# Rank products of four-tile groups, a gate product and one narrowing operation put at other places of a hand-written order

## The chip, the cores and the metric

The kernel runs on one core of a Trainium2 chip. The metric is device time in microseconds (us), the median of three runs. The core has a matmul engine (PE, with its weight loads as PEld), a vector engine (DVE), a scalar engine (ACT), GpSimd (POOL) and SyncE (SP), which mostly issues transfers (DMA). Each engine works through its own instructions in order and waits for the others on semaphores.

## What is computed

A gated linear attention over 4 batches, 8 heads, 768 positions of width 40; then a mixture of 8 experts (3072 tokens of width 320), of which each token takes at most one; then a block with three weights, a maximum over the three products, and an output product.

```python
# attention, per head and position t
m_new = maximum(f + m, i)
C = exp(f + m - m_new) * C + exp(i - m_new) * outer(v, k)
n = exp(f + m - m_new) * n + exp(i - m_new) * k
y = sigmoid(o) * (C @ q) / maximum(abs(n @ q), 1)
# experts: only tokens with x @ w_skip > 0
e = argmax(xc @ w_gate); gate = softmax(xc @ w_gate)[e]
out = xc + gate * (maximum(xc @ w1[e], 0) @ w2[e])
# final block
h = maximum(maximum(x @ w1, x @ w2), x @ w3)
return h @ w_out
```

## The kernel before, in words

**Tiles and turns.** The attention is cut into 6 chunks of 128 positions times 4 batches: 24 tiles, numbered 0 to 23, tile i being chunk i // 4 and batch i % 4. The loop `for i in range(NT)` (L1221) is a software pipeline; one pass is called a turn here. Nothing reorders it: each engine's instructions stand in the order in which the code emits them. Turn i holds, in this order,
- SP's loads of tile i+2 (`load`, TP at L872 and KP at L874) and of the gate rows;
- `score(i+1)` (PE L900, with DVE's products W, L908) and `keys(i+1)` (POOL kt, L915);
- the previous tile's `last` (POOL XR, L988);
- `state_mm(i)` (PE L929), the first half of `pv_mm` (PE L965), `expo_mm` (PE L882, L890, ACT L891), `inter_mm` (PE L936);
- `state(i)`: DVE xi (L946), POOL Cst (L949: the state of one batch times its decay), DVE Cst (L954: two adds onto it);
- the second half of `expo_mm`, then rank and gate products when they are due, then the second half of `pv_mm`;
- `logit` (PE L1015), `trans(i-1)` (PE L1000: the previous tile's XR is transposed into bank mi, ACT xTH L1002 and DVE xTL L1005 read it);
- a scatter (POOL L1118) if one is pending, two in turns 20 and later;
- a *weave*: several runs of small DVE operations, one operation of each in turn: `finish` (DVE xs L972, den L978 to L982, then POOL g L985), `narrow`, xTL (L1005), and what the routing or the gates need.

A turn in the trace is taken below from the first L900 of `score(i+1)` to the next one's. Turn 6 begins at 55.38 us, turn 16 at 129.46, turn 20 at 155.98, turn 21 at 161.72, turn 22 at 171.98; the first product of the final block (L322) is at 181.69.

**Routing.** Tiles 0 to 15 are routed in groups of four, tiles 16 to 23 in pairs. When a group's logits are there, its next turns run `route2` (DVE: which expert) and then `route3_mm` and `route3` (L1080 to L1107): PE sums one-hot rows into each token's rank among its expert's tokens, in bank mi; ACT copies the ranks (rk); five small DVE operations make the row numbers si and the place column of XR; POOL adds the group's counts to cum (L1091). Then each tile of the group is scattered: an indirect DMA that writes 128 rows of `table` in device memory. After the attention the experts gather their tokens from `table`.

**The early read.** In turn 20 `early_load` (SP L289) reads 512 rows of `table`, those of tokens that take no expert, for the final block, whose first products are put into the last turns. The rows that it needs come from the first 12 tiles (`assert issued[0] >= SNAP`). It is the only read of `table` in the attention.

**Narrowing.** Weights of the final block come in as pieces of 128x384 double-width numbers (mraw, DMA issued by ACT, L210). DVE packs a piece into single width in three operations: L224, L226 and, a turn later, L239 (`narrow2`). ACT then takes the high part (mH, L246), POOL the remainder (mL or oL, L252, `mp.low`, called behind `state`).

**Gates.** For the next chunk a gate product (`gating3`, PE L848 to L850 into bank mi, ACT copies KG and DEC, L851 and L852) comes once in four turns: turns 5, 9, 13, 17 from the second chunk on.

Of the kernel before, what the change touches and what calls it, by code (L numbers as in the profile page):

```python
# [20 lines left out]
NC = S // NB  # L21
# [30 lines left out]
def bc(ap, shape):  # L52
    return ap.to_broadcast(shape)
# [587 lines left out]
def attention(k, tp, kp, og, gates, w9, wts, left, mp, moe):  # L641
    tc, nc = k.tc, k.nc
    rows, table, ident, zrow = k.rows, k.table, k.ident, k.zrow
    with ExitStack() as ctx:
# [291 lines left out]
                    nc.tensor.matmul(t["pi"][:, 2 * j : 2 * j + 2].rearrange("p a d -> p (a d)"), t["TP"][:, 0, j],  # L936
                                     Cst[:, b, j], start=True, stop=True)

        def state(i):
            t = st[i]  # L940
            c, b = t["c"], t["b"]
            Cb = Cst[0:104, b]
            pc = t["pc"]
            if c > 0:
                t["xi"] = xi = pt2.tile([128, H, D1], F32, name="xi", bufs=1)
                nc.vector.tensor_mul(xi, t["pi"], bc(KG[c % 2][:, 1, b * H : (b + 1) * H].unsqueeze(2), [128, H, D1]))  # L946
            if c < NC - 1:
                if c > 0:
                    nc.gpsimd.tensor_mul(Cb, Cb, bc(DEC[c % 2][:, b].unsqueeze(2), [104, 4, 2 * D1]))  # L949
                for q in range(2):  # L950
                    r = slice(64 * q, 64 * q + D)
                    w = Cb[r, :, q * D1 : (q + 1) * D1]
                    if c > 0:
                        nc.vector.tensor_add(w, w, pc[r])  # L954
                    else:
                        nc.vector.tensor_copy(w, pc[r])
# [193 lines left out]
                todo.append(r)  # L1150

        todo = []
        rts = [None, None]


        early = {}
# [64 lines left out]
        for i in range(NT):  # L1221
            c = i // B
            if i > 0 and i + 2 < NT:
                load(i + 2)
            if i % B == 2 and c + 1 < NC:
                loado(c + 1)
            if i % B == 0 and 0 < c and c + 1 < NC:
                rowout(c + 1)
            if B <= i + 3 < NT:
                rowin(i + 3)  # L1230
            if i == 1:
                w9load()
            if i == 3:
                w9split()
            if i < E:
                pads(i)
            if i == NT - 4:
                early_load()
            rts = [todo.pop() if todo else None, rts[0]]
            if i + 1 < NT:  # L1240
                score(i + 1)
                keys(i + 1)
            if i > 0:
                st[i - 1]["last"]()
            state_mm(i)
            pv_mm(i, 0)
            if i == NT - 1:
                tail2(i - 2)
                rts[0] = todo.pop()
            if i == NT - 2:  # L1250
                early_prep(0)
                early_prep(1)
            if i + 2 < NT:
                expo_mm(i + 2, 0)
            if i + 1 == NT:
                early["run"] = mixed_block(k, mp, early["x"], early["xt"], T2, early_tile)
                fill(1)
            inter_mm(i)
            state(i)
            mp.low()  # L1260
            if rts[0]:
                route2_mm(rts[0])
            if i + 2 < NT:
                expo_mm(i + 2, 1)
            if i == 0:
                sigm(0)
            if rts[1] and i < NT - 2:
                route3_mm(rts[1])
            if i % B == 1 + (c == 0) and c + 1 < NC:
                gating3(c + 1)  # L1270
            if i % B == 3 and c + 1 < NC:
                sigm(c + 1)
            pv_mm(i, 4)
            if rts[1] and i >= NT - 2:
                route3_mm(rts[1], "pl" if i == NT - 1 else "mi")
            if 1 < i < NT - 1:
                tail2(i - 2)
            if i > 0:
                tail1(i - 1)
            mp.load(min(i + 1, 4))  # L1280
            scatter()
            if i >= NT - B:
                scatter()
            runs = [finish(i, xr(i)), mp.narrow(PIECES[i])]
            if i > 0 and "low" in st[i - 1]:
                runs.append(st[i - 1]["low"])
            if i % B == (c == 0) and c + 1 < NC:
                runs.append(gating2(c + 1))
            if i == NT - 1:
                fill(2)  # L1290
                weave(*runs[:2])
                next(st[i - 1]["low"])
                st[i]["last"]()
                fill(1)
                tail1(i)
                fill(1)
                runs = [st[i]["low"]]
            if rts[0]:
                runs.append(route2(rts[0]))
            if rts[1]:  # L1300
                runs.append(route3(rts[1]))
            if i % B == (c == 0) and c + 2 < NC:
                runs.append(gating(c + 2))
            if i % B == 1 + (c == 0) and c + 2 < NC:
                runs.append(gating1(c + 2))
            if i == NT - 2:
                next(runs[0])
                next(st[i - 1]["low"])
                early_prep(2)
                early_prep(3)  # L1310
            weave(*runs)
            if i % B == (c == 0) and c + 2 < NC:
                gload(c + 3)
# [81 lines left out]
```

## Time and profile before

| | us |
|---|---|
| median of three runs | 587.95 (586.24, 587.95, 590.15) |
| profiled execution | 588.96 |
| its span, first to last instruction | 587.2 |
| attention, turns 6 to 20 | 55.38 to 161.72 |
| turns 21 and 22 | 161.72 to 181.69 |
| turn 23 and what is left of the routing, beside the first final blocks | 181.69 to 206.00 |
| experts | 206.00 to 340.00 |
| the final block | 340.00 to 587.20 |

Over the span PE is busy 547.4 us (93%), DVE 314.1 (53%), ACT 235.6, POOL 229.0. An average over stages says little: what an edit is worth is read in its own stage. In the rows below a time is the instruction's start; the number in brackets is how long its engine stood idle before it, and behind the arrow is what released it. DMA-issuing instructions of SP and ACT are marked SPq and ACTq.

### The profile page before, as it was taken

The numbers are of one execution on the slowest core, as the hardware profiler recorded it, in microseconds if no ns is written. First come the engines' busy times: TensorE is split into PE (matmuls) and PEld (weight loads), VectorE is DVE, ScalarE is ACT, GpSimd is POOL, SyncE is SP. The second block draws the span as 40 slices with busy tenths as digits, with TensorE's granted clock in tenths as the row PEclk, the third lists the DMA queues.
The fourth block names the chain that finished last, engine by engine and source line by source line (L and its number), as shares of the span: only waits on it lengthen the run. The fifth ranks groups of instructions, "written<-read, shape, count | busy, mean of one in ns | idle before, by whom it ended". The sixth has DMA issues, their size and how long they took to land.

```text
span 587.2 us, 10688 instructions
## 1 busy us (share of the span) xinstructions
PE 547.4 (93%) x3890; PEld 478.1 (81%) x3890; DVE 314.1 (53%) x786; ACT 235.6 (40%) x505; POOL 229.0 (39%) x271
## 2 busy tenths in 40 slices
PE   7978988989979998999999999999999999999990
PEld 4866777777868778999999988898898898898890
DVE  7768989998866673677787532312212311311210
ACT  5554645554622333768677422221222222222120
POOL 4325667687754442242424412131231232132231
PEclk9989988999979999999999999999999999999996
DMA  6687877687740137569887511010001001000000
GB/s 224 179 284 229 285 232 221 221 271 226 237 150 23 47 110 249 171 196 308 250 284 251 157 56 55 0 46 1 1 35 56 1 33 58 1 24 23 0 25 27
DMA packets 38631, 77.01 MB, mean 131 GB/s; under 512 B 6446, under 2 KB 20783, under 8 KB 38568
## 3 DMA queue, kind: packets, MB, share of 16 engines
q1 hardware_dynamic: 27528, 57.33, 30.9%
q10 hardware_dynamic: 8064, 9.05, 5.1%
q0 software_dynamic: 2976, 9.85, 4.4%
q8 instruction: 33, 0.54, 0.4%
q14 instruction: 30, 0.25, 0.1%
HBM read 63.30 MB, written 13.27 MB: 130 GB/s over the span
## 4 chain that ended last, share of the span: by engine, by line
PE 71%; DVE 11%; DMA 7%; issue 3%; POOL 3%; ACT 2%; SPq 0%; ACTq 0%; POOLq 0%; DVEq 0%
PE pd L322 17%; PE ps L322 17%; PE pd L471 6%; PE pv L965 3%; PE ps L404 3%; DMA mraw<-m 2%; DMA SA<-rows 2%; DMA TP<-tp 2%; PE pv L426 1%; PE pv L428 1%; PE ic L427 1%; PE ic L428 1%; PE ic L426 1%; PE pv L427 1%; PE ps L900 1%
## 5 line engine op out<-in xcount | busy, mean ns | idle before, releaser
L303 POOL TENSOR_TENSOR hL<-t,hH 128x512 fp32r<-128x512 f32 x30 | 38.6, 1288 | 141.5 <-ACT hH L302 141.5
L161 DVE TENSOR_TENSOR w<-raw,w 128x768 fp32r<-128x768 f32 (+1 forms) x48 | 48.5, 1037 | 14.3 <-ACT w L160 14.3
L965 PE MATMUL pv<-KP,W 128*128 128x123 f32 (+2 forms) x384 | 55.2, 290 | 0.1
L302 ACT CAST hH<-t 128x512 fp32r<-128x512 f32 x30 | 18.6, 621 | 90.5 <-DVE t L312 90.5
L160 ACT CAST w<-raw 128x768 fp32r<-128x768 f32 (+1 forms) x64 | 49.2, 786 | 13.3 <-DMA raw<-w 8.2
L965 PEld LDWEIGHTS pv<-KP,W 128*128 128x128 f32 x384 | 49.8, 200 | 3.4 <-DVE xs L972 0.4
L311 DVE TENSOR_TENSOR t<-t,ps 128x512 f32<-128x512 f32 x15 | 10.3, 688 | 64.3 <-PE ps L322 64.2
L322 PE MATMUL ps<-fxH,mH 128*128 128x512 f32 x108 | 43.3, 401 | 0.0
L322 PE MATMUL pd<-fxH,mH 128*128 128x512 f32 x108 | 43.0, 399 | 0.0
L322 PE MATMUL ps<-fxH,mL 128*128 128x512 f32 x108 | 42.8, 396 | 0.0
L322 PE MATMUL pd<-fxH,mL 128*128 128x512 f32 x108 | 42.8, 396 | 0.0
L985 POOL TENSOR_TENSOR g<-O,den 128x320 f32<-128x320 f32 x24 | 19.9, 829 | 58.1 <-DVE den L982 36.0
L891 ACT ACTIVATE W<-pd 128x512 f32<-128x512 f32 x48 | 27.9, 592 | 27.5 <-PE pd L890 21.3
L471 PE MATMUL pd<-xT,w 128*128 128x256 f32 x288 | 37.8, 283 | 0.0
L900 PE MATMUL ps<-TP 64*128 64x128 f32 x384 | 30.7, 301 | 6.5 <-DMA TP<-tp 4.3
L471 PEld LDWEIGHTS pd<-xT,w 128*128 128x128 f32 x288 | 35.4, 188 | 0.2 <-DVE hL L475 0.2
L900 PEld LDWEIGHTS ps<-TP 64*128 64x128 f32 x384 | 25.8, 201 | 11.0 <-DVE den L982 3.0
L432 POOL DMA_INDIRECT table<-y,xb x14 | 14.3, 1023 | 52.2 <-DMA raw<-w 13.5
L161 POOL TENSOR_TENSOR w<-raw,w 128x640 fp32r<-128x640 f32 x16 | 25.2, 1580 | 20.1 <-ACT w L160 20.0
L908 DVE TENSOR_TENSOR W<-ps,W 128x512 f32<-128x512 f32 x48 | 30.5, 675 | 1.4 <-PE ps L900 1.0
L344 POOL DMA_INDIRECT out<-o,fx x20 | 19.6, 982 | 28.4 <-ACT o L343 26.9
L1118 POOL DMA_INDIRECT table<-XR,si x24 | 24.6, 1023 | 11.6 <-DVE xi L946 5.2
(376 smaller groups left out, 1498.0 us busy)
## 6 DMA issues: line engine op xcount, KB each, us to landing
TP<-tp SPq DMA_DIRECT2D x24, 512.0 KB
raw<-w SPq DMA_DIRECT2D x32, 384.0 KB
raw<-w SPq DMA_DIRECT2D x32, 320.0 KB
KP<-kp SPq DMA_DIRECT2D x24, 324.0 KB
mraw<-m ACTq DMA_DIRECT2D x18, 384.0 KB
O<-og SPq DMA_DIRECT2D x6, 640.0 KB
fx<-table SPq DMA_DIRECT2D x5, 642.0 KB
table<-zrow SPq DMA_DIRECT2D x8, 323.0 KB
```

What stands on the lines that cost most here:

```text
L160: nc.scalar.copy(hi, r)
L161: (nc.gpsimd if m and s % 2 else nc.vector).tensor_sub(lo, r, hi.bitcast(F32))
L303: nc.gpsimd.tensor_sub(g, t, h.bitcast(F32))
L322: nc.tensor.matmul(p, w, z, start=i == 0, stop=i == len(tt) - 1)
L344: ins = nc.gpsimd.indirect_dma_start(k.out, bass.IndirectOffsetOnAxis(ap=x.bitcast(I32)[:, j + q, IDC : IDC + 1], axis=0), o, None, bounds ...
L471: nc.tensor.matmul(ps[:, f], w, x, start=f == 0 and i == 0, stop=f == 1 and i == 7)
L891: nc.scalar.activation(st[i]["W"][:, q], pd, AF.Exp)
L900: nc.tensor.matmul(ps[q][:, j], TP[r, 1, j], TP[r, 0, j], start=True, stop=True)
L908: nc.vector.tensor_mul(t["W"][:, q], t["ps"][q], t["W"][:, q])
L965: nc.tensor.matmul(t["pv"][:, h:h1], t["W"][:, h % 2, h // 2], t["ve"][:, h:h1], start=True, stop=True)
L985: nc.gpsimd.tensor_mul(g, sg[c][:, b], bc(den.unsqueeze(2), [128, H, D]))
L1118: ins = nc.gpsimd.indirect_dma_start(table, bass.IndirectOffsetOnAxis(ap=si, axis=0), x, None, bounds_check=ROWS - 1, oob_is_err=False)
```

## The change

- The rank products (`route3_mm`) and the DVE work behind them (`route3`) of a group of four come a turn later: in turns 8, 12, 16 and 20, where they stood in 7, 11, 15 and 19. In that turn the rank products stand right behind `score` and `keys`, ahead of `state_mm`; before, they stood behind the second half of `expo_mm`. Groups of two keep their turns.
- The scatters follow: those of tiles 0 to 15 come a turn later, and from turn 19 on (one turn sooner) two may go in a turn. So tiles 10 and 11 both go in turn 19, turn 20 has no scatter (before, those of tiles 12 and 13), and turns 21 and 22 have the two each of the next group.
- `gating3` stands in turns 6, 10, 14 and 18, where it stood in 5, 9, 13 and 17.
- `narrow` is made ahead of `state`, and its first operation, an L239 where a piece is half packed, comes between xi and the state's adds (turns 4 to 21, 18 times). The rest of its operations move one place up in the weave. A piece that leaves the list sooner lets `mp.load` fetch the following one a turn sooner: turn 4 issues two, and all later ones are a turn early.

```diff
-        def state(i):
+        def state(i, other):
...
                 nc.vector.tensor_mul(xi, t["pi"], bc(KG[c % 2][:, 1, b * H : (b + 1) * H].unsqueeze(2), [128, H, D1]))
+                if mp.mid:
+                    next(other, None)
...
-            rts = [todo.pop() if todo else None, rts[0]]
+            rts = [todo.pop() if todo else None, rts[0], rts[1]]
+
+            if rts[2] and rts[2]["nb"] < 4:
+                rts[2] = None
+            if rts[1] and rts[1]["nb"] == 4:
+                ranked = None
+            else:
+                ranked = rts[1] or rts[2]
             if i + 1 < NT:
                 score(i + 1)
                 keys(i + 1)
+            if rts[2]:
+                assert not rts[1]
+                route3_mm(rts[2])
...
-            state(i)
+            narrowing = mp.narrow(PIECES[i])
+            state(i, narrowing)
...
-            if rts[1] and i < NT - 2:
-                route3_mm(rts[1])
-            if i % B == 1 + (c == 0) and c + 1 < NC:
+            if ranked and not rts[2] and i < NT - 2:
+                route3_mm(ranked)
+            if i % B == 2 and c + 1 < NC:
                 gating3(c + 1)
...
-            if i >= NT - B:
+            if i >= NT - B - 1:
                 scatter()
-            runs = [finish(i, xr(i)), mp.narrow(PIECES[i])]
+            runs = [finish(i, xr(i)), narrowing]
...
-            if rts[1]:
-                runs.append(route3(rts[1]))
+            if ranked:
+                runs.append(route3(ranked))
```

Line numbers of the changed kernel are higher by two from the second line of `state`'s adds on (L1118 is L1120 there).

POOL at turns 19 to 21, before. The first row is the scatter of turn 19; the two waiting for DMAHW1, the transfer of the early read, are those of turn 20.

```order
L1118 DMA table<-XR,si 28672x323
L1091 TENSOR_TENSOR cum<-cum,oh 128x4x9 [waits DVE_49,PE_49,Activation_49]
L985 TENSOR_TENSOR g<-O,den 128x320 [waits DVE_49,Pool_49]
L988 TENSOR_TENSOR XR<-xs,g 128x320 [waits Pool_49]
L252 TENSOR_TENSOR oL<-mtmp,oH 128x320 [waits Activation_49]
L1118 DMA table<-XR,si 28672x323 [waits DMAHW1_49,DVE_49,Activation_49]
L1118 DMA table<-XR,si 28672x323
L985 TENSOR_TENSOR g<-O,den 128x320 [waits DVE_49,Pool_49]
L988 TENSOR_TENSOR XR<-xs,g 128x320 [waits DMASW2_49,DMASW1_49,DMASW3_49,DMASW0_49,Pool_49]
```

The same place of the changed kernel:

```order
L1120 DMA table<-XR,si 28672x323 x2
L987 TENSOR_TENSOR g<-O,den 128x320 [waits DVE_49,Pool_49]
L990 TENSOR_TENSOR XR<-xs,g 128x320 [waits Pool_49]
L252 TENSOR_TENSOR oL<-mtmp,oH 128x320 [waits Activation_49]
L1093 TENSOR_TENSOR cum<-cum,oh 128x4x9 [waits PE_49]
L987 TENSOR_TENSOR g<-O,den 128x320 [waits DVE_49,Pool_49]
L990 TENSOR_TENSOR XR<-xs,g 128x320 [waits DMASW2_49,DMASW1_49,DMASW3_49,DMASW0_49,Pool_49]
L252 TENSOR_TENSOR oL<-mtmp,oH 128x320 [waits Activation_49]
L1120 DMA table<-XR,si 28672x323 [waits DMAHW1_49,DVE_49,Activation_49]
```

The second g and the second XR (those of tile 20) stood behind two scatters that wait for the early read; now the first scatter that waits for it stands behind them.

PE at turns 7 and 8, before: the rank products (L1080 to L1084) of the first group, in turn 7, stand between `expo_mm` and `pv_mm`.

```order
L936 MATMUL ic<-Cst,TP 128x82 x4
...
L890 MATMUL pd<-SM,SA 128x512 [waits DMAHW4_49]
L1080 LDWEIGHTS tri [waits DVE_49,PE_49]
L1080 MATMUL mi<-oh,tri 128x36 [waits Activation_49]
...
L1084 MATMUL mi<-oh,ones 128x9
L965 MATMUL pv<-KP,W 128x123 x2
```

In the changed kernel they stand in turn 8, behind the eight products of `score(9)`:

```order
L1002 MATMUL mi<-ident,XR 128x128 x2
L900 MATMUL ps<-TP 128x128 [waits DMAHW7_49,DVE_49]
L900 MATMUL ps<-TP 128x128 [waits DVE_49]
L900 MATMUL ps<-TP 128x128 x6
L1082 LDWEIGHTS tri
L1082 MATMUL mi<-oh,tri 128x36 [waits DVE_49]
...
L1086 MATMUL mi<-oh,ones 128x9
L929 MATMUL ic<-KP,kt 40x41 [waits DMAHW6_49]
```

Their first product now waits for DVE alone: bank mi was written by the transposes L1002 just ahead, and DVE's xTL is the last to read it. All of `state_mm`, `pv_mm` and `inter_mm` stands behind that wait.

DVE in a turn that prepares a gate (turn 5), before:

```order
L908 TENSOR_TENSOR W<-ps,W 128x512 x2
L946 TENSOR_TENSOR xi<-ic,KG_121 128x328
L954 TENSOR_TENSOR Cst<-Cst,ic 40x4x41 x2
L972 TENSOR_TENSOR xs<-xi,pv 128x328
L239 SCALAR_TENSOR_TENSOR mtmp<-mraw,mtmp 128x384
L1005 TENSOR_TENSOR xTL<-mi,xTH 128x3x128
```

and in the changed kernel:

```order
L908 TENSOR_TENSOR W<-ps,W 128x512 x2
L946 TENSOR_TENSOR xi<-ic,KG_121 128x328
L239 SCALAR_TENSOR_TENSOR mtmp<-mraw,mtmp 128x384
L956 TENSOR_TENSOR Cst<-Cst,ic 40x4x41 x2
L974 TENSOR_TENSOR xs<-xi,pv 128x328
L239 SCALAR_TENSOR_TENSOR mtmp<-mraw,mtmp 128x384
L1007 TENSOR_TENSOR xTL<-mi,xTH 128x3x128
```

One L239 stands between xi and the adds. Here a second piece is half packed, and its L239 keeps the place behind xs; in most turns there is only the first.

## Rows read from the trace of the kernel before

**Rows 1.** Windows: stretch, length, then busy us (instructions) of PE PEld DVE ACT POOL; PEclk; DMA; GB/s.

```profile
55.38:161.72 106.34, 97.02 (x1034) 82.53 (x1034) 96.61 (x289) 58.40 (x121) 75.65 (x93) 0.97 0.77 241
```

**Rows 2.** Waits of DVE, 55.38 to 161.72 us: us in total, times, longest.

```profile
DVE Cst L954 <- POOL Cst L949: 6.0, 8, 1.3
```

**Rows 3.** Waits of PE, 55.38 to 161.72 us.

```profile
PE mi L1080 <- DVE sm L1068: 3.4, 3, 1.6
PE mi L848 <- DVE R L842: 2.0, 2, 1.2
```

**Rows 4.** Windows: turns 9, 11, 13, 21 and 22.

```profile
77.16:85.47 8.31, 8.31 (x73) 7.13 (x73) 7.60 (x22) 2.03 (x6) 5.84 (x7) 0.79 0.73 233
...
91.43:101.05 9.62, 8.00 (x79) 6.55 (x78) 9.22 (x28) 5.03 (x9) 8.13 (x11) 0.84 0.63 189
...
106.73:114.74 8.01, 6.83 (x75) 5.74 (x74) 7.95 (x24) 3.39 (x9) 5.76 (x7) 1.00 0.55 180
...
161.72:171.98 10.26, 6.54 (x60) 5.32 (x59) 5.93 (x24) 2.87 (x8) 4.64 (x6) 0.89 0.55 181
171.98:181.69 9.71, 9.71 (x72) 9.08 (x72) 6.70 (x22) 3.42 (x13) 6.52 (x8) 0.76 0.19 70
```

**Rows 5.** Timeline, turns 19 to 22: start, us, engine line op; idle before in brackets.

```profile
155.93 1.01 POOL L1118 DMA_INDIRECT table<-XR,si  x1 [0.15 <-issue]
...
161.46 0.40 SPq L289 DMA_DIRECT2D ex<-table  x1
...
161.97 0.44 SPq L872 DMA_DIRECT2D TP<-tp  x1
...
163.83 0.20 DVE L982 RECIPROCAL den<-den 128x8 f32<-128x8 f32 x1
...
167.16 1.01 POOL L1118 DMA_INDIRECT table<-XR,si  x1 [5.15 <-DVE xi L946]
...
168.48 0.98 POOL L1118 DMA_INDIRECT table<-XR,si  x1 [0.30 <-issue]
169.48 0.74 POOL L985 TENSOR_TENSOR g<-O,den 128x320 f32<-128x320 f32 x1
170.29 0.81 POOL L988 TENSOR_TENSOR XR<-xs,g 128x320 f32<-128x320 f32 x1
...
171.16 0.90 PE L1000 MATMUL mi<-ident,XR 128*128 128x128 f32 x3 [3.72 <-POOL XR L988]
```

**Rows 6.** Timeline of DVE and POOL: L239 in turns 6 and 7.

```profile
60.76 1.95 POOL L252 TENSOR_TENSOR mL<-mtmp,mH 128x384 fp32r<-128x384 f32 x2
...
61.93 1.20 DVE L239 SCALAR_TENSOR_TENSOR mtmp<-mraw,mtmp 128x384 int32<-128x384 int32 x1
...
70.01 0.55 DVE L239 SCALAR_TENSOR_TENSOR mtmp<-mraw,mtmp 128x384 int32<-128x384 int32 x1
```

**Rows 7.** Timeline of PE and DVE, turn 16.

```profile
129.46 1.16 PE L900 MATMUL ps<-TP 64*128 64x128 f32 x16
...
131.00 0.55 DVE L1005 TENSOR_TENSOR xTL<-mi,xTH 128x384 fp32r<-128x384 f32 x1
...
131.47 0.19 DVE L1096 TENSOR_TENSOR sl<-rk,ebase 128x36 f32<-128x36 f32 x1
...
132.41 1.02 PE L936 MATMUL ic<-Cst,TP 128*128 128x82 f32 x8
...
134.14 0.49 DVE L946 TENSOR_TENSOR xi<-ic,KG 128x328 f32<-128x328 f32 x1
```

**Rows 8.** Timeline of PE behind three of its waits, turns 9, 11 and 13.

```profile
77.16 1.74 PE L900 MATMUL ps<-TP 64*128 64x128 f32 x16 [1.89 <-DVE mtmp L239]
...
97.44 0.18 PE L1080 MATMUL mi<-oh,tri 128*128 128x36 bf16 x1 [1.62 <-DVE sm L1068]
...
97.65 1.19 PE L965 MATMUL pv<-KP,W 128*128 128x123 f32 x6
...
112.31 0.32 PE L848 MATMUL mi<-R,sel 32*104 32x16 f32 x2 [1.18 <-DVE R L842]
```

More of the change, by code (lines that the diff above doesn't have):

```diff
@@ L1152, in attention @@
         todo = []
-        rts = [None, None]
+        rts = [None, None, None]
         early = {}
@@ L1273, in attention @@
             pv_mm(i, 4)
-            if rts[1] and i >= NT - 2:
-                route3_mm(rts[1], "pl" if i == NT - 1 else "mi")
+            if ranked and not rts[2] and i >= NT - 2:
+                route3_mm(ranked, "pl" if i == NT - 1 else "mi")
             if 1 < i < NT - 1:
```

## The prediction

> **What bounds the kernel now.** I read the windows by stage first. The experts and the final block, from 206 us on, keep their instructions and their order, so what the change can move lies before 181.69 us. In turns 6 to 20 PE is busy 97.0 and DVE 96.6 of 106.3 us [rows 1], so busy shares don't say which of them sets the pace. The waits do. DVE idles 106.3 - 96.6 = 9.7 us, and 6.0 of it is the state's adds (L954) waiting for POOL's product Cst, eight times, at most 1.3 us [rows 2]. PE's waits mostly end with a small DVE operation [rows 3]: PE runs ahead, reaches a product whose input DVE hasn't made, and stands. So DVE sets the pace of turns 6 to 20, and a wait of PE costs nothing there as long as DVE has work queued.
>
> Then I read the turns one by one. Turn 21 takes 10.26 us with PE busy 6.54, and turn 22 9.71 with PE busy throughout at a granted clock of 0.76 [rows 4]: little work, much time. The timeline says why [rows 5]. PE ends its last product at 167.44 and stands 3.72 us until 171.16, released by POOL's XR of tile 20. That XR starts at 170.29, behind g at 169.48, although g's input den was there from 163.83 + 0.20. POOL was held by turn 20's scatter, which started at 167.16 after 5.15 us idle. The releaser named is xi, but xi had long been done; in the order that scatter waits for the early read of `table`. SP issued that read only at 161.46, because it waits for turn 19's scatter, issued at 155.93, to land (5.5 us). A chain of two transfers thus stood in POOL's queue ahead of two products that didn't need them.
>
> **Part 1a, scatters: turn 20's hole.** In the changed order g and XR of tile 20 stand ahead of the first scatter that waits for the early read. I follow the new chain. den is ready at 164.03, g takes 0.74 and XR 0.81 with starts 0.81 apart: XR ends about 164.1 + 0.8 + 0.8 = 165.7, and releases nothing late. PE ends its logits at 167.44, transposes at once, and could start the next score about 168.0 instead of 171.98. The next limit is that score's TP: SP issues it behind the early read (161.97 [rows 5]), which now waits for the second scatter of turn 19. In rows 5 two scatters start 1.32 us apart, so everything of SP there comes 0 (if the earlier scatter had slack) to 1.3 us later. Before, TP must have landed by 171.98; the early read had landed by 167.16, when the scatter went, and TP was issued 0.51 behind it, so about 167.7 before and up to 169.0 after. The gain is 171.98 less 168.0 to 169.0: **3.0 to 4.0 us**.
>
> Behind the wait of 3.72 us, turn 22 ran at 0.76. Its work at full clock is 9.71 x 0.76 = 7.4, say 7.6 us: a further **2.1 us** if no long wait comes before it. A wait of 0.6 to 1.6 us stays. The rows have one of 1.18 us, behind which the three gate products passed in 0.4 us and turn 13, with it, ran at 1.00; one of 1.62 us in turn 11, which ran at 0.84; and one of 1.89 us, behind which the score took 1.74 us where it takes 1.16 in turn 16, and turn 9 ran at 0.79 [rows 8, 4, 7]. The middle of the new wait, 1.1, is nearest to 1.18, so I take 2.1, with 0.6 as the lower end. Together 3.6 to 6.1; I take **-5.6**, near the upper end because the wait lies nearer to the row without a fall.
>
> The scatters themselves aren't saved. Two move from turn 20 to 21 and two from 21 to 22, and those of turn 23 come later; POOL is busy 4.64 of 10.26 us in turn 21 [rows 4], so they find room: 0.
>
> **Part 1b, rank products behind the score.** Before, they wait for DVE's sm at the end of a turn (3.4 us in three turns [rows 3]). That wait goes, and a new one comes: bank mi must be free of the last transposes, which DVE's xTL reads. Turn 16 shows it [rows 7]: the score ends at 129.46 + 1.16 = 130.62, xTL at 131.55. So PE would stand 0.93 us, then the eight rank products, which take 0.2 (97.44 to 97.65 [rows 8]). Behind them in PE's queue are `state_mm`, the first `pv_mm` and `inter_mm`; all shift by about 1.2 us. The shift reaches DVE's xi: L936 ends at 133.43 + 1.2 = 134.6, where xi started at 134.14. And xi itself could start some 0.5 earlier, since the five rank operations, of up to 0.19 us each and overlapping [rows 7], have left the weave ahead (0.5 is my estimate): DVE waits about 1.0. But in these turns DVE's adds waited for POOL anyhow: up to 1.3 us, 0.75 a time over the eight of rows 2, and the turns with the long ones follow a routing turn. The wait moves from the adds to xi and is paid once. Bounds: 0 (all covered) to 4 x 1.2 = +4.8 (none); by the longest hole of rows 2, 0. **I take +0.4**: three turns covered by a long hole, and one with a hole of the mean, 0.75, where 1.2 - 0.75 is left.
>
> **Part 2, gates a turn later.** Three small products leave turns where PE waited for them (2.0 us in two turns [rows 3]) and go where PE has its inputs. PE's waits there weren't on DVE's path, so removing them earns 0; the new place adds some 0.4 us to a PE that runs ahead of DVE: 0, bounds -0.4 x 4 to +0.4 x 4.
>
> **Part 3, L239 ahead of the adds.** It looks like 18 x 0.55 us of work put into waits. The rows speak against that. The adds wait for POOL's Cst, a product of two operands in SBUF. L239 also reads two such operands, and while POOL's L252 pair ran (60.76 to 62.71) an L239 took 1.20 us instead of the 0.55 of turn 7 [rows 6]: it got through when POOL's instruction let it. An L239 put beside Cst is served before it or after it, and the adds wait for both. So the hole isn't filled with free time: what L239 gains, Cst loses. On the other side L239 leaves the place behind xs, where it sometimes met L252. Bounds per turn: -0.55 x 8 turns with holes = -4.4 if it hid fully, and +0.55 x 4 = +2.2 where the wait for Cst was nil and L239 now delays adds that others wait for. By the 1.20 row I take **0**.
>
> The Trainium skill says the same as a rule (SBUF — State Buffer, "Who interferes with whom"): a DVE instruction with two SBUF inputs contends with a GpSimd instruction that reads SBUF, and whoever starts first holds the shared ports for the whole instruction. By that rule L239 in the hole is serialised with Cst; without it one would write -4.4 here. The 1.20 beside 0.55 agrees with it.
>
> The earlier fetch of one 384 KB piece in turn 4 competes once with TP; DVE is behind there. Bounds 0 and, if it costs PE what a late TP cost turn 9 [rows 8], +1.9; I take 0. Later pieces each come a turn early, which fills no wait in the rows.
>
> **Sum.** 588.96 - 5.6 + 0.4 + 0 + 0 + 0 = 583.8 for an execution like the profiled one. That was 1.0 above the median of the runs, so **582.8**. Lower end of this case: -6.1, and -1 for parts 2 and 3, 580.9; upper end: -3.6 and +1.5, 585.9.
>
> **Rivals.**
> - *L239 does hide, and PE's clock recovers.* The holes are filled (-4.4 at most, half of it likely, since a hole of 0.75 holds one L239) and the wait for sm behind which turn 11 ran at 0.84 is gone: 9.62 x 0.16 = 1.5 us of PE. For it: L239 may start before Cst in the short gap in which POOL still does XR. Against: 1.20 in rows 6, and DVE, not PE, is behind. 582.8 - 2.2 to -4: about **579.5**.
> - *The new waits lower PE's clock.* A stand of 0.9 to 1.5 us four times lies between the 1.18 that didn't drop it and the 1.62 that did [rows 8]. Each drop costs what turn 9 lost, 8.31 x 0.21 = 1.7 us [rows 4]. For it: the wait is repeated, and it adds to PE's other waits in the turn. Against: DVE is behind and hides a part. Two to four drops, +3.4 to +6.8: about **587**, no change that can be told.
> - *The gain is handed on.* TP or the early read comes later than reckoned, PE stands over 1.6 us in turn 21 and stays slow in turn 22: -1.5 to -2: about **586.5**.
> - *Slower.* The wait for mi at `tri` in turns 8, 12, 16 and 20 isn't 0.9 but 2.4 us, because DVE runs xTL late in its weave behind a longer queue. Then each turn loses the clock (1.7) and the 1.2 that the Cst hole can't cover: 4 x 2.9 = 11.6, against the 5.6 won: 588.96 + 6.0 - 1.0 = **594**. It decides where the clock falls in all four, between 1.18 and 1.62 us of wait a turn: four times 1.7 already outweighs the 5.6. Against: in turn 16 DVE's xTL is 0.4 behind the end of the score; before the score's end it has little else to do.
>
> **How the numbers follow.** About 1% (5.9 us) is what a measurement of this kernel can tell from no change. The forecast's case gets 0.60, the hidden L239 0.13, the lowered clock 0.15, the gain handed on 0.06, slower 0.06. Below 582.1 lie 0.13 and half of the forecast's case: faster 0.43. Above 593.8: slower 0.06. The rest, 0.51, is the same. The range leaves out the slowest case and the ends of the two outer ones: 579.0 to 588.5.
>
> **What would show it.** Right: turn 21 lasts about 6.5 to 7.5 us and turn 22 about 7.6 at a clock near 1; g and XR of tile 20 stand on POOL ahead of any scatter and end before 167; the rank products wait about 1 us for xTL, and in those turns the adds no longer wait for Cst; L239 ahead of the adds takes about 0.55 to 1.2 with Cst delayed as much. Wrong: turns 6 to 20 together differ from 106.3 us by more than 2, one way by filled holes, the other by clocks under 0.9 in turns 8, 12, 16 and 20; or turn 22 still at 0.76.

## The result, and the profile after

The changed kernel takes 593.57 us (median of 11 runs, 591.08 to 597.0), the kernel before 587.95 (11 runs, 585.49 to 590.15): ratio 1.0103, interval 1.0074 to 1.0132. It is slower by 1%, where I had forecast 582.8 us and given a slower kernel 6 in 100. The profiled execution after takes 591.08 us, the shortest of its eleven, and that of before 588.96, one above its median: the two traces show 2.1 us of the 5.6 that the medians differ by. What single edits cost is therefore read from medians below, and the traces show where.

Windows of after: turns 6 to 20, then turns 8, 9, 10, 12, 21 and 22 (a turn from the first L900 of its score, as before).

```profile
54.92:169.65 114.73, 101.95 (x1038) 86.29 (x1038) 101.65 (x284) 58.92 (x122) 76.41 (x93) 0.96 0.69 222
...
69.24:75.70 6.46, 5.83 (x71) 5.21 (x71) 5.16 (x13) 3.41 (x6) 3.61 (x5) 1.00 0.77 273
75.70:83.70 8.00, 6.59 (x71) 5.42 (x70) 7.96 (x26) 3.54 (x9) 3.94 (x7) 1.00 0.51 165
83.70:93.97 10.27, 10.16 (x71) 8.50 (x72) 8.79 (x19) 4.10 (x11) 6.97 (x8) 0.67 0.62 203
...
100.61:110.24 9.63, 7.97 (x71) 6.88 (x71) 6.68 (x16) 4.69 (x7) 5.74 (x7) 0.82 0.56 182
...
169.65:176.97 7.32, 6.14 (x60) 5.13 (x59) 7.05 (x27) 2.66 (x9) 4.27 (x5) 1.00 0.51 184
176.97:184.70 7.73, 7.65 (x73) 7.06 (x72) 6.99 (x23) 3.67 (x14) 4.70 (x7) 1.00 0.17 60
```

Turns 21 and 22 together are 4.9 us shorter than in [rows 4], much as forecast. Turns 6 to 20 are 8.4 us longer than in [rows 1]: DVE is busy 5.0 us longer there with the same work and idles 13.1 us instead of 9.7.

Waits of DVE, and the first wait of PE, over the same stretch of after:

```profile
DVE xi L946 <- PE ic L936: 7.5, 5, 2.9
DVE Cst L956 <- POOL Cst L951: 3.4, 3, 1.4
...
PE mi L1082 <- DVE xTL L1007: 5.2, 4, 1.6
```

The wait of the adds is 3.4 us where [rows 2] has 6.0. In its place stands a wait of xi for PE of 7.5 us, and PE waits 5.2 us for xTL in front of the moved rank products. Turn 12 has all of it (timeline of PE, DVE and POOL):

```profile
103.91 0.18 PE L1082 MATMUL mi<-oh,tri 128*128 128x36 bf16 x1 [1.55 <-DVE xTL L1007]
...
108.74 0.50 DVE L946 TENSOR_TENSOR xi<-ic,KG 128x328 f32<-128x328 f32 x1 [2.87 <-PE ic L936]
108.79 0.73 POOL L951 TENSOR_TENSOR Cst<-Cst,DEC 104x328 f32<-104x328 f32 x1 [1.75 <-PE ic L936]
...
109.16 1.74 DVE L239 SCALAR_TENSOR_TENSOR mtmp<-mraw,mtmp 128x384 int32<-128x384 int32 x1
...
109.48 1.01 POOL L252 TENSOR_TENSOR mL<-mtmp,mH 128x384 fp32r<-128x384 f32 x1
...
110.82 0.65 DVE L956 TENSOR_TENSOR Cst<-Cst,ic 40x164 f32<-40x164 f32 x2
```

PE stands 1.55 us for xTL; everything behind it comes later, at a granted clock of 0.82, so xi waits 2.87 us. In turn 16, behind the same wait of 1.55 us but at a clock of 1.00, xi waits 1.22 us. POOL's Cst waits for the same products of PE. L239 starts while Cst runs, and behind Cst follows L252 without a gap: L239 takes 1.74 us, and the adds, whose Cst was ready at 109.52, start at 110.82. Turn 10, in which the clock was 0.67, has the longest one:

```profile
91.40 0.50 DVE L946 TENSOR_TENSOR xi<-ic,KG 128x328 f32<-128x328 f32 x1 [1.43 <-PE ic L936]
91.44 0.73 POOL L951 TENSOR_TENSOR Cst<-Cst,DEC 104x328 f32<-104x328 f32 x1 [0.65 <-PE ic L936]
91.82 2.70 DVE L239 SCALAR_TENSOR_TENSOR mtmp<-mraw,mtmp 128x384 int32<-128x384 int32 x1
...
92.14 1.97 POOL L252 TENSOR_TENSOR mL<-mtmp,mH 128x384 fp32r<-128x384 f32 x2
...
94.44 0.65 DVE L956 TENSOR_TENSOR Cst<-Cst,ic 40x164 f32<-40x164 f32 x2
```

L239 takes 2.70 us, beside 0.55 in [rows 6], through Cst and both L252; the adds start 2.3 us behind Cst's end. Over turns 6 to 20 the L239 sum to 16.9 us after and 12.7 before.

### The profile page after: what moved, and what is told of

It reads as the page before. It is cut to its first block, busy times and chain, and to the rows that moved or that the text cites. A ratio compares the mean times of both kernels' runs of the same rounds, so it can differ in the third digit from the quotient of the medians.

```text
span 589.4 us, 10680 instructions
## 1 busy us (share of the span) xinstructions
PE 549.2 (93%) x3890; PEld 478.8 (81%) x3890; DVE 321.8 (55%) x786; ACT 235.7 (40%) x505; POOL 229.3 (39%) x271
## 4 chain that ended last, share of the span: by engine, by line
PE 71%; DVE 17%; issue 4%; DMA 2%; POOL 2%; ACT 2%; ACTq 0%; POOLq 0%; SPq 0%; DVEq 0%
PE pd L322 17%; PE ps L322 17%; PE pd L471 6%; PE pv L967 3%; PE ps L404 3%; DVE W L908 2%; DVE xTL L1007 2%; PE pv L428 1%; PE ic L426 1%; PE pv L427 1%; PE ic L427 1%; PE ic L428 1%; PE pv L426 1%; PE ic L936 1%; DVE mtmp L224 1%
## 5 line engine op out<-in xcount | busy, mean ns | idle before, releaser
L987 POOL TENSOR_TENSOR g<-O,den 128x320 f32<-128x320 f32 x24 | 17.9, 746 | 64.3 <-DVE den L984 47.2
L891 ACT ACTIVATE W<-pd 128x512 f32<-128x512 f32 x48 | 27.9, 592 | 27.8 <-PE pd L890 21.7
L900 PE MATMUL ps<-TP 64*128 64x128 f32 x384 | 31.7, 292 | 6.9 <-DVE den L982 2.2
L900 PEld LDWEIGHTS ps<-TP 64*128 64x128 f32 x384 | 25.9, 192 | 12.1 <-DVE W L908 3.8
L432 POOL DMA_INDIRECT table<-y,xb x14 | 14.3, 1023 | 51.9 <-ACT w L160 13.1
L161 POOL TENSOR_TENSOR w<-raw,w 128x640 fp32r<-128x640 f32 x16 | 25.2, 1579 | 20.3 <-ACT w L160 20.2
L322 PE MATMUL pd<-fxL,mH 128*128 128x512 f32 x72 | 28.5, 396 | 0.0
```

The lines of the kernel that those rows point to most:

```text
L161: (nc.gpsimd if m and s % 2 else nc.vector).tensor_sub(lo, r, hi.bitcast(F32))
L322: nc.tensor.matmul(p, w, z, start=i == 0, stop=i == len(tt) - 1)
L891: nc.scalar.activation(st[i]["W"][:, q], pd, AF.Exp)
L900: nc.tensor.matmul(ps[q][:, j], TP[r, 1, j], TP[r, 0, j], start=True, stop=True)
L987: nc.gpsimd.tensor_mul(g, sg[c][:, b], bc(den.unsqueeze(2), [128, H, D]))
```

## The experiments

Seventeen kernels, each timed in five rounds beside the kernel before on the same chip. Times are medians, ratios are to the kernel before with their intervals; its median was 585.7 to 586.3 us in these rounds. Each kernel is named by its label. Differences between kernels are taken from the ratios, 0.1% being 0.6 us.

### The parts alone

**s_skip**: before, with no scatter in turn 20.

```diff
-            scatter()
-            if i >= NT - B:
-                scatter()
+            if i != NT - B:
+                scatter()
+            if i > NT - B:
+                scatter()
```

> The kernel before with one edit: turn 20 issues no scatter (its two go in turn 21, and so on). Theory A (the shorter turns 20 to 22 of the changed kernel come from the scatter that no longer stands in POOL's queue ahead of tile 20's g and XR): turns 20 to 22 together 4 to 6 us shorter, 582 to 584 us, turns 6 to 19 as before. Rival (they come from the other parts, or PE waits for TP instead): no more than 1 us off 588.

582.87 us, 0.9944 (0.9916 to 0.9972): a gain of 3.3 us. Its trace has turns 20 to 22 at 19.55 us instead of 25.71; tile 20's XR no longer waits behind a scatter. Timeline of s_skip:

```profile
158.33 0.41 SPq L289 DMA_DIRECT2D ex<-table  x1
...
162.82 0.83 POOL L988 TENSOR_TENSOR XR<-xs,g 128x320 f32<-128x320 f32 x1
...
164.63 1.02 POOL L1118 DMA_INDIRECT table<-XR,si  x1 [0.16 <-PE pv L965]
...
165.12 0.49 PE L1000 MATMUL mi<-ident,XR 128*128 128x128 f32 x3
```

PE's transposes of XR start with no wait, and the scatter stands behind XR. The mechanism is the forecast one; the price is another matter (below).

**g_only**: before, with gating3 a turn later.

```diff
-            if i % B == 1 + (c == 0) and c + 1 < NC:
+            if i % B == 2 and c + 1 < NC:
                 gating3(c + 1)
```

> The kernel before with gating3 one turn later, and nothing else. Theory A: no effect, 587 to 589. Rival (the products lengthen the turns they move to): 590 to 592.

585.38 us, 0.9949 (0.9914 to 0.9983): faster, which neither theory had. In its trace PE no longer waits for R, as it did in two turns [rows 3], and waits up to 1.26 us for ACT ahead of the same products instead. The scatter order is still the old one here, so its trace shows the old stall in turn 21 in a second execution:

```profile
157.42 0.40 SPq L289 DMA_DIRECT2D ex<-table  x1
...
162.63 1.02 POOL L1118 DMA_INDIRECT table<-XR,si  x1 [2.41 <-ACT oh L1061]
...
165.77 0.81 POOL L988 TENSOR_TENSOR XR<-xs,g 128x320 f32<-128x320 f32 x1
166.64 0.55 PE L1000 MATMUL mi<-ident,XR 128*128 128x128 f32 x3 [0.99 <-POOL XR L988]
```

The same scatter stands ahead of the same XR, but PE waits 0.99 us and not 3.72 as in [rows 5], and turns 20 to 22 take 21.33 us. In this execution the early read was issued 2.5 us before turn 21's score (159.93), in that of before 0.3 us, and the scatter that waits for it went 5.2 us behind the issue, there 5.7.

**n_only**: before, with L239 between xi and the adds (the two lines of `state` and the argument `narrowing`, as in the change).

> The kernel before with one L239 put between xi and the state's adds, and nothing else of the change. Theory A (L239 loses the race for the ports to POOL's Cst and then to L252 behind it, and the adds wait for it): several L239 of 1.2 to 2.7 us, 589 to 592 us. Rival 1 (the long L239 only come where PE's new wait makes xi late): 587 to 588.5. Rival 2 (it hides in the adds' waits, as hoped): 584 to 586.

587.87 us, 1.001 (0.9981 to 1.004): the time is rival 1's, but without any new wait of PE two L239 of 1.73 us stand in its trace, in turns 5 and 8, both where Cst had itself waited for late products of PE; the others are at most 1.05 us. Turns 20 to 22 take 21.69 us, with PE waiting 1.28 us for XR, again with the old scatter order.

**r_only**: before, with rank products and scatters as in the change (gates and L239 at their old places).

> The kernel before with the rank products and scatters of the changed kernel, gates and L239 at their old places. Theory A (PE's wait for xTL delays xi by more than the adds' old waits cover, the last turns win 5 us): turns 8, 12, 16 longer by 0.5 to 2 us each, turns 20 to 22 shorter by 5: 584 to 588. Rival (the rank products are covered as forecast, all of the loss is L239's): 582.5 to 584. Rival 2 (rank products make all of the loss): 592 to 594.

592.99 us, 1.009 (1.006 to 1.012): rival 2, nearly the whole loss, although the scatters' gain is in it. It also has gating3 directly behind the rank work, where PE waits 1.49 and 1.60 us for DVE in turns 9 and 13; the change moves gating3 away from there, so this loss is larger than the rank products' share in the changed kernel (a_no_n, below, differs from r_only by the gates alone and is 0.44% faster).

**gs**: before, with the edits of s_skip and g_only together.

> The kernel before with two edits: gating3 a turn later, and no scatter in turn 20. Both gains are there and add up: 578 to 582 us. Rival (they are the same gain, both by a PE clock that stays up in turns 20 to 22): 582 to 584.

582.22 us, 0.9922 (0.9893 to 0.9951). Between the two: the gates add 0.2% to the scatters' 0.6%, less than alone, and 0.2% is within the uncertainty. This is the base for what follows: the changed kernel less the rank work's move and less L239's. (Its scatters only skip turn 20; those that come a turn later belong to the rank work's move.)

### One thing put back into the changed kernel, or added to the base

**late_no_n**: the base, with the rank work a turn later but at its old place in the turn.

```diff
-            if rts[2]:
-                assert not rts[1]
-                route3_mm(rts[2])
...
-            if ranked and not rts[2] and i < NT - 2:
+            if ranked and i < NT - 2:
                 route3_mm(ranked)
```

(The diff is against the changed kernel; n_only's lines are taken out as well.)

> The changed kernel with the rank products at their old place in the turn (behind expo_mm, still in turns 8, 12, 16, 20) and L239 back in the weave: it differs from the kernel with the two gains (582) only by the rank work being a turn later. Theory W: 581 to 583. Rival (the rank work in one weave with the gates' chain costs by itself): 584 to 586.

585.75 us, 0.9988 (0.9965 to 1.0011): the rival. The rank work a turn later costs 0.67% of the time, 3.9 us, though no product waits for xTL any more.

**a_no_n**: the changed kernel with L239 back in the weave. It differs from late_no_n only by the early place in the turn.

> The changed kernel with L239 back in the weave. Theory A (behind PE's wait xi is late, L239 meets Cst and L252 and takes 1.7 us, and the adds wait for it): 588 to 591, 3 to 5 us less than the changed kernel. Rival (L239 costs nothing, as it did alone): 592 to 594.

588.37 us, 1.0046 (1.0014 to 1.0078): theory A, 3.3 us less than the changed kernel. Against late_no_n the early place costs 0.58%, 3.4 us.

**a_late**: the changed kernel with the rank products at their old place in the turn (late_no_n's diff, L239 as changed).

> The changed kernel with the rank products of groups of four in the same turns (8, 12, 16, 20), but at their old place in the turn, behind the second half of expo_mm instead of right behind score. Theory W (PE's wait for xTL ahead of state_mm is what costs): no wait at their first product, xi waits under 0.5 us in those turns, 580 to 584 us. Rival (the rank work a turn later costs wherever it stands, by its DVE part or its scatters): 589 to 593.

588.37 us, 1.0035 (1.001 to 1.006): between the two, nearer to the rival. The early place costs 0.68% here, 4.0 us; the rest of the loss stays.

**gs_n**: the base with L239 ahead of the adds.

> The kernel with gates later and no scatter in turn 20, and L239 ahead of the adds. Theory A (L239 meets Cst and L252 wherever PE is late, and costs by itself): 584 to 587, with two or more L239 over 1.5 us. Rival (it costs only beside the rank products' wait): 581 to 583.

583.92 us, 0.9963 (0.9938 to 0.9987): 2.4 us more than the base, just under theory A. Only one L239 over 1.5 us stands in its trace, 2.70 us in turn 6.

**gs_wait**: the base, with one tiny product into bank mi behind score, which waits for xTL as the moved rank products do.

```diff
                 keys(i + 1)
+            if i in (8, 12, 16, 20):
+                nc.tensor.matmul(k.bank("mi", [128, 4, E + 1])[:, 0], tri, cum[:, 0, 0 : E + 1], start=True, stop=True)
```

> The kernel with gates later and no scatter in turn 20, and one tiny extra product into bank mi right behind score in turns 8, 12, 16 and 20, whose result nobody reads; the rank products stay in turns 7, 11, 15, 19. It measures the wait for xTL alone. Theory W (the wait ahead of state_mm costs by itself): PE waits 0.6 to 1.6 us there, xi 1 to 2.5, 585 to 588 us, 3 to 6 more than without it (582). Rival (the turn of the rank work costs, not the wait): 581 to 583.

582.25 us, 0.9921 (0.9892 to 0.9949): the rival, no cost at all. Timelines of turn 8 in gs_wait, and of turn 12 in a_no_n, which has the real products there:

```profile
73.17 0.18 PE L1244 MATMUL mi<-cum,tri 128*128 128x9 bf16 x1 [1.09 <-DVE xTL L1005]
...
76.19 0.50 DVE L946 TENSOR_TENSOR xi<-ic,KG 128x328 f32<-128x328 f32 x1 [0.41 <-PE ic L936]
77.47 0.66 DVE L954 TENSOR_TENSOR Cst<-Cst,ic 40x164 f32<-40x164 f32 x2 [0.77 <-POOL Cst L949]
```

```profile
103.99 0.18 PE L1080 MATMUL mi<-oh,tri 128*128 128x36 bf16 x1 [1.28 <-DVE xTL L1005]
...
107.17 0.50 DVE L946 TENSOR_TENSOR xi<-ic,KG 128x328 f32<-128x328 f32 x1 [1.03 <-PE ic L936]
108.04 0.66 DVE L954 TENSOR_TENSOR Cst<-Cst,ic 40x164 f32<-40x164 f32 x2 [0.36 <-POOL Cst L949]
```

PE waits 1.09 and 1.28 us, xi 0.41 and 1.03, the adds 0.77 and 0.36. Waits of xi and adds together are 1.18 and 1.39 us, and [rows 2] had up to 1.3 at the adds alone: in these turns the wait is indeed paid once. It isn't always: in turn 8 of a_no_n, at a granted clock of 0.79, PE waits 0.95 us and xi 2.37. In gs_wait, with one product in place of eight, the wait of PE by itself costs nothing.

**a_pv**: the changed kernel with the rank products in spare columns of bank pv, free at DVE's xs, ahead of xTL.

```diff
+                st[i]["pvb"] = k.bank("pv", [128, 512])
-                route3_mm(rts[2])
+                route3_mm(rts[2], st[i]["pvb"])
...
-                t["pv"] = k.bank("pv", [128, H, D1])
+                b = t["pvb"] if "pvb" in t else k.bank("pv", [128, 512])
+                t["pv"] = b[:, 0 : H * D1].rearrange("p (h d) -> p h d", h=H)
```

> The changed kernel with the rank products in spare columns of bank pv instead of bank mi, at the same place: they wait for DVE's xs, which comes some 0.7 us before xTL. Theory W: PE's wait in turns 8, 12 and 16 about 0.7 us shorter each, and a third to a half of the loss comes back: 587 to 591. Rival (the place, not the wait): 592 to 595.

591.7 us, 1.0083 (1.0052 to 1.0114). It lies between theory and rival, and its interval overlaps that of the changed kernel: undecided. PE's waits in turns 8, 12, 16 and 20 are 0.81 us, none, 0.82 and 0.75, where the changed kernel has 0.63, 1.55, 1.55 and 1.45; halving them brought back no loss that can be told.

**a_low**: the changed kernel with `mp.low()` (POOL's L252) behind the scatter.

> The changed kernel with POOL's L252 behind the scatter instead of right behind Cst. Theory A (L239 of 1.7 and 2.7 us wait for Cst and for the L252 that follows it without a gap): no L239 over 1.3 us, adds no later than Cst's end, 1 to 4 us less than the changed kernel: 589 to 592. Rival (L239 is held by Cst alone): L239 as long as before, 592 to 595.

606.76 us, 1.0341 (1.0311 to 1.0371): a miss on all counts. Timeline of turn 10 of a_low:

```profile
86.74 1.52 POOL L1120 DMA_INDIRECT table<-XR,si  x1 [0.18 <-issue]
...
87.48 2.22 DVE L239 SCALAR_TENSOR_TENSOR mtmp<-mraw,mtmp 128x384 int32<-128x384 int32 x1
88.29 1.00 POOL L252 TENSOR_TENSOR mL<-mtmp,mH 128x384 fp32r<-128x384 f32 x1
...
89.64 0.65 DVE L956 TENSOR_TENSOR Cst<-Cst,ic 40x164 f32<-40x164 f32 x2
...
90.43 0.78 PE L929 MATMUL ic<-KP,kt 128*40 128x41 f32 x16 [2.07 <-DVE Cst L956]
```

L239 now starts while the scatter is being issued, runs on through L252, and ends 2.22 us later; the adds come late. And the adds free bank ic: PE's `state_mm` of the next turn (L929) waits 2.07 us for them. That is a second path by which a late L239 costs, and the changed kernel seems to have it too (0.96 us in turn 18, until 0.1 us behind the end of the adds; the profile names no releaser on DVE there).

### Why the rank work a turn later costs

**late_bal**: late_no_n, with the gates' six DVE operations (gating) a turn earlier. By the code they stand in turns 4, 8 and 12 and move to 3, 7 and 11; the rank work has left 7 and 11. (The expectations here count these turns as 8, 12 and 16 and as 7, 11 and 15; in turn 16 there is no gating, only the one DVE operation that makes R.)

```diff
-            if i % B == (c == 0) and c + 2 < NC:
-                runs.append(gating(c + 2))
+            if i == 1:
+                runs.append(gating(2))
+            if i % B == 3 and c + 3 < NC:
+                runs.append(gating(c + 3))
```

> The kernel with the rank work a turn later behind expo_mm and L239 in the weave (585.8), with one more edit: the six DVE operations that prepare the next-but-one chunk's gates (gating) stand in turns 7, 11 and 15 instead of 8, 12 and 16. Theory B (the rank work a turn later falls into the turn whose weave already holds the gates' chain, DVE's fullest turn, so den and with it POOL's g, XR and PE's transposes come later): the reciprocal of den in the turn behind is back at about 3.1 us behind the score's start from 4.3, 581 to 584 us. Rival (it is something else of the rank work a turn later: its scatters, its ACT copy): 585 to 587.

582.88 us, 0.9949 (0.9921 to 0.9977): theory B, 2.3 us less than late_no_n. The end of turn 13 in late_no_n, then in late_bal:

```profile
113.66 0.76 DVE L799 TENSOR_TENSOR nm<-AM,Fc 32x1 f32<-32x1 f32 x1
...
114.41 1.27 DVE L908 TENSOR_TENSOR W<-ps,W 128x512 f32<-128x512 f32 x2
...
114.46 0.55 PE L1000 MATMUL mi<-ident,XR 128*128 128x128 f32 x3 [1.63 <-POOL XR L988]
...
115.13 0.29 PEld L900 LDWEIGHTS ps<-TP 64*128 64x128 f32 x2 [0.37 <-DVE W L908]
115.14 1.75 PE L900 MATMUL ps<-TP 64*128 64x128 f32 x16
...
115.73 0.96 PEld L900 LDWEIGHTS ps<-TP 64*128 64x128 f32 x14 [0.30 <-DVE W L908]
```

```profile
113.77 1.27 DVE L908 TENSOR_TENSOR W<-ps,W 128x512 f32<-128x512 f32 x2
...
114.58 0.55 PE L1000 MATMUL mi<-ident,XR 128*128 128x128 f32 x3 [0.54 <-POOL XR L988]
...
115.06 1.19 PE L900 MATMUL ps<-TP 64*128 64x128 f32 x16
```

With both in one weave PE waits 1.63 us for POOL's XR, and the score behind it takes 1.75 us: at a granted clock of 1.00, but both its halves wait for DVE's W (0.37 and 0.30 us), which stands behind the gates' L799 and starts 7.49 us into turn 13. With gating moved W starts 5.64 us into that turn, PE waits 0.54 us, and the score takes 1.19. The reciprocal of turn 10 ended 4.31 us behind the score's start in late_no_n, 3.72 in late_bal and 2.64 in the base: part of the way, not the forecast 3.1. Whether the base too would gain from an earlier gating was not tried.

**late_r3end**: late_no_n, with the five rank operations behind the rest of the weave.

```diff
-                runs.append(route3(ranked))
...
             weave(*runs)
+            if ranked:
+                weave(route3(ranked))
```

> The same kernel (585.8) with the five rank operations of DVE behind the rest of the weave instead of in turn with it. Theory C (they only push back the reciprocal inside the weave): 582 to 584. Theory B (DVE's fullest turn is too full, in whatever order): 585 to 587.

585.62 us, 1.0 (0.9972 to 1.0027), as late_no_n: theory C falls. The order inside the weave isn't the cost; that the turn has too much for DVE is what is left of the two theories.

**late_bal_19**: late_bal, with the fourth group's rank work back in turn 19.

```diff
-            if rts[2] and rts[2]["nb"] < 4:
+            if rts[2] and (rts[2]["nb"] < 4 or rts[2]["i0"] == 12):
                 rts[2] = None
-            if rts[1] and rts[1]["nb"] == 4:
+            if rts[1] and rts[1]["nb"] == 4 and rts[1]["i0"] < 12:
```

(turn 20 again without a scatter)

> The kernel with the first three groups' rank work a turn later behind expo_mm, gating in turns 7, 11 and 15, L239 in the weave (582.9), and the fourth group's rank work back in turn 19. Theory D: turns 20 to 22 at 19.5 to 20.5 us instead of 22.0, 579.5 to 581.5. Rival: 582 to 584.

581.8 us, 0.9908 (0.9876 to 0.9939), and turns 20 to 22 take 19.71 us instead of 22.01: theory D, the time 0.3 us above its range. It is the fastest kernel of the study, equal to the base within the intervals, and it beats both kernels of the case. So the first three groups' rank work a turn later costs nothing that can be told, once it doesn't meet the gates' chain and the fourth group's doesn't meet the first pair's routing. What the fourth group's met in turn 20 (timelines of late_no_n, then of the base):

```profile
166.70 0.72 DVE L1107 TENSOR_TENSOR XR<-rk,plc 128x4 int32<-128x4 f32 x1
...
167.54 0.77 DVE L1062 TENSOR_TENSOR fm<-fm,cm 128x2 f32<-128x2 f32 x1
...
168.34 0.80 DVE L1064 TENSOR_TENSOR oh<-em,fm 128x16 bf16<-128x16 f32 x1
...
169.29 0.17 PE L1080 MATMUL mi<-oh,tri 128*128 128x18 bf16 x1 [1.41 <-DVE sm L1068]
```

```profile
162.99 0.40 DVE L1062 TENSOR_TENSOR fm<-fm,cm 128x2 f32<-128x2 f32 x1
...
163.41 0.18 DVE L1064 TENSOR_TENSOR oh<-em,fm 128x16 bf16<-128x16 f32 x1
```

Pushed back by the rank operations, the pair's small operations fall beside POOL's XR and L252 and take 0.77 and 0.80 us where the base has 0.40 and 0.18; PE, in turn 21, waits 1.41 us for the pair's sm. All kernels with the fourth group in turn 20 and no scatter there have turns 20 to 22 at 22.0 to 25.2 us, those without it 19.5 to 20.4.

**a_bal** and **a_19**: the changed kernel with late_bal's and with late_bal_19's edit.

> The changed kernel with gating in turns 7, 11 and 15. Theory B: 588 to 591, some 3 to 4 us less than the changed kernel; what is left is L239's and the early place's. Rival: 592 to 595.

590.95 us, 1.0097 (1.0059 to 1.0136): in theory B's range by its time, but by the ratio only 0.06% below the changed kernel.

> The changed kernel with the rank products of the fourth group (tiles 12 to 15) back in turn 19 at their old place; turn 20 still has no scatter. Theory D (in turn 20 the rank work meets the first pair's routing in one weave, sm comes late and PE waits for it in turn 21; this eats what the scatters' move won): turns 20 to 22 together 19.5 to 20.5 us instead of 22.6, 2 to 3 us less than the changed kernel: 589.5 to 591.5. Rival (turns 20 to 22 are as they are for another reason): 22 to 23 us there, 592 to 594.

592.78 us, 1.0111 (1.008 to 1.0143). In its trace turns 20 to 22 take 20.04 us instead of 22.57, as theory D has it, but no gain is in the median, and the intervals of both leave open whether there is one. With L239 and the early place in the kernel these two repairs can't be told from nothing; why, I did not settle.

## Why the prediction was wrong

By medians the loss adds up from neighbours that differ by one edit: base 0.9922; rank work a turn later +0.67% (late_no_n); the early place +0.58% (a_no_n); L239 +0.57% (the changed kernel, 1.0103). The last two in the other order are +0.47% (a_late) and +0.68%. Each step has an uncertainty of some 0.4%; their sum, 1.8%, is far outside it. The steps hold along this path: taken back in the changed kernel alone, the two meetings of the rank work brought nothing that can be told (a_bal, a_19).

**Part 1a, scatters, -5.6 us: mechanism right, size wrong.** POOL's order was what held XR, and turns 21 and 22 of the changed kernel are 4.9 us shorter than in the trace of before (turn 20, which the fourth group's rank work enters, is 1.8 us longer). But the stall of 3.72 us was one execution's. Two others with the old order, of kernels with one other edit each (g_only, n_only), waited 0.99 and 1.28 us, kept a clock of 1.00 and needed 21.3 and 21.7 us for turns 20 to 22, against 19.5 with the scatters moved. The gain is about 2 us by those traces and 3.3 by the medians; I had priced one bad execution, with its 2.1 us of clock, as the usual one.

**Part 1b, rank products, +0.4 us: the step that failed.** The wait for xTL was foreseen, with its size (0.93 us and the products; 0.63 to 1.55 came), and that it is paid once in place of the adds' wait is borne out by gs_wait, whose turns ran at a clock of 1.00. What failed is a term that wasn't in the sum: I priced the five DVE operations as moved at no cost, "have left the weave ahead", and never asked which weave they enter. They enter those of turns 8 and 12, with the gates' chain, that of turn 16, and that of turn 20, with the first pair's routing; DVE, the engine that I had named as setting the pace, is full there: in the windows of after it is busy 7.96 of 8.00 us in turn 9, where turn 8's weave runs, behind 5.16 of 6.46 in turn 8, where the rank operations would have had room. late_bal and late_bal_19 take out these two meetings, and in a kernel without the early place and L239's move the 3.9 us are gone.

The early place costs another 3.4 to 4.0 us on top, in a kernel where the rank work is late already; the wait alone, in the base, costs nothing (gs_wait). The waits of PE and xi in turn 12 of a_no_n, 1.28 and 1.03 us, are longer than in gs_wait; turn 12 of the changed kernel shows 1.55 and 2.87 with the clock at 0.82. That the clock gives a part of the difference agrees with all executions: their mean granted clock is 0.980 in late_no_n and 0.975 in a_no_n, 0.979 in a_late and 0.976 in the changed kernel, each difference just outside its uncertainty of 0.004. Over the executions of the kernel before, 0.001 less of clock went with 0.36 us more, so I estimate 1.9 of the 3.4 us and 1.4 of the 4.0 for the clock. What makes the rest no run separates. The other two steps went without a lower clock: 0.978 in the base and 0.980 in late_no_n, 0.975 in a_no_n and 0.976 in the changed kernel.

**Part 2, gates, 0: too low.** They gain 0.5% alone, and beside the scatters 0.2%, which is within the uncertainty. That removing PE's waits there earns 0 doesn't hold for the kernel before; by which path the gain comes no run separates.

**Part 3, L239, 0: mechanism half seen.** I had L239 and Cst serialised, and where L239 comes first that holds: in a_late the adds wait 1.39 us, five times, with L239 ahead of them, no less than the 1.3 of [rows 2]. I didn't look at what stands behind Cst on POOL. L252 follows without a gap, and an L239 that loses to Cst loses to L252 as well. That happens where xi is late: in turns 8, 12 and 16 of the changed kernel behind part 1b's wait, in turn 10 at the lowered clock. Alone the edit costs 0.1% (n_only, within the uncertainty), on the base 0.4%, in the changed kernel 0.6%.

But a_late pays 0.47% with only one L239 over 1.2 us in turns 6 to 20 (2.90 us in turn 6). A second cost shows in the traces with the edit: the rest of `narrow` stands one place higher in the weave too, and there L224 falls beside L252. Turn 7 of the changed kernel:

```profile
60.83 1.96 POOL L252 TENSOR_TENSOR mL<-mtmp,mH 128x384 fp32r<-128x384 f32 x2
...
62.00 1.00 DVE L224 TENSOR_SCALAR mtmp<-mraw 128x384 int32<-128x384 int32 x1
```

L224 takes 1.00 us, where 0.35 is usual. Over turns 6 to 20 it sums to 7.9 to 8.6 us in after, a_late, gs_n and n_only, and to 6.3 to 6.6 in before, gs, gs_wait, late_no_n and a_no_n. What these 1.5 us of DVE are worth no run separates.

**The rivals.** The time came out where the slower rival put it, 594, and one of its places was right, the wait for mi; that the number agrees is luck. Its mechanism wasn't there: it needs 2.4 us of wait and a lowered clock in all four turns; the waits were 0.63, 1.55, 1.55 and 1.45, and of the four turns only turn 12 had a lowered clock (and turn 10, which has no such wait). The waits of 1.55 came once with 0.82 and once with 1.00, so their length alone didn't decide. a_low shows what that rival describes: waits of 1.55, 2.59, 2.58 and 2.13 us, clocks of 0.81, 0.70, 0.71 and 0.83 in these turns, and 606.76 us. The loss had three sources of about equal size, two of which no rival named.

## What to carry to other kernels

An operation moved to another turn isn't free because its instructions are the same: look up what the turn that it enters already holds on the engine that sets the pace, and whether that engine reaches its next urgent result later. Before a stall is priced as a gain, look for it in a second execution: a stall that hangs on when a transfer lands was three to four times as long in the trace at hand as in two others. And an instruction put into a wait must be checked against everything that follows the awaited one on the other engine, not against the awaited one alone.

## What the runs showed of the hardware

A DVE instruction that finds POOL at work on SBUF can be held through POOL's following instructions as well: L239 took 2.70 us through Cst and two L252 in turn 10, 1.74 through the end of Cst and one L252 in turn 12, and ended 0.41 us behind the last L252 both times; [rows 6] has 0.55. The Trainium skill (SBUF — State Buffer, "Who interferes with whom") has whoever issues first hold the shared ports for the whole instruction; the rows agree, and show besides that the next POOL instruction got in ahead of a DVE instruction already waiting. In a_low L224, a shift with one input in SBUF, took 2.24 us, where 0.3 to 0.4 is usual: from the end of a scatter's issue on through two L252, ending 0.23 us behind the second:

```profile
96.56 1.01 POOL L1120 DMA_INDIRECT table<-XR,si  x1 [0.16 <-issue]
...
97.54 2.24 DVE L224 TENSOR_SCALAR mtmp<-mraw 128x384 int32<-128x384 int32 x1
97.60 1.95 POOL L252 TENSOR_TENSOR mL<-mtmp,mH 128x384 fp32r<-128x384 f32 x2
```
